# Hash-bucket attention and experts on one core: batch 0 visited once in float32, a planner that knows shared PSUM banks, Z beside the values

## The chip, the cores and the metric

One core of a Trainium2 chip. The metric is the device time of one execution in microseconds (us), as the median of several runs. A profile comes from one further execution; its span, from the first to the last instruction, lies a little inside its own time.

## The reference

Attention over q, k, v of shape (4 batches, 8 heads, 768, 64). `proj` gives each query and key a 6-bit bucket by the signs of six products; a query sees only the keys of its own bucket. The output of all heads, as 3072 tokens of 512, goes through one expert layer of 2048.

```python
mask = q_bucket[:, :, :, None] == k_bucket[:, :, None, :]
scores = np.where(mask, scale * np.matmul(q, k.transpose(0, 1, 3, 2)), -1000000000.0)
scores = scores - np.max(scores, axis=-1, keepdims=True)
attn = np.exp(scores)
attn = attn / (np.sum(attn, axis=-1, keepdims=True) + 1e-09)
x = np.matmul(attn, v)            # then (B, S, H * D) as B * S tokens
h = x @ w_in
g = s * (np.maximum(h, 0.0) ** 2) + b
return g @ w_out
```

## The kernel before

Work is cut into **slots**: one head of one batch and a chunk of 256 of its 768 queries, 96 slots in all. A **visit** is a head with the chunks that are done in a row. In a slot, `scores` writes 6 key tiles of scores into three PSUM banks (leading products, line 537 in float32, line 539 in float32r, a format with fewer passes), VectorE takes the maximum over tiles (L544), TensorE transposes it into bank 4 (L548), VectorE reduces it (L550), TensorE transposes back (L552), VectorE writes a row of negative maxima (L558), a closing product adds it to the scores (L567 or L569), and ACT takes the exps (L574). `values` multiplies exps by v into bank 3 (L596 float32; L598 and L599 for exps split into two float32r halves by ACT L591 and POOL L592). The sum of exps, Z, comes from a column of ones beside v and a spreading matmul (L614, L615), from 64 columns of ones (L617), or from VectorE and a float32r product (L620 to L626). ACT reads Z and the values from the banks (L628, L630), VectorE adds the low half (L632). For two heads together follow a reciprocal (L636) and a write of x to a buffer in DRAM (`xd`).

**Batch 0** is visited twice. First come eight visits with chunk 0 alone, all in float32 from tiles EQ and EK, one pair per head, which lie in the space of the weights' later halves. Then eight visits with chunks 1 and 2: `resplit` makes float32r halves of the head's q and k (ACT L446 and L453, POOL L448 and L456, six DMAs), so scores are float32r, while exps and v stay float32. Batches 1 to 3 are visited head by head with three chunks, in float32r halves throughout; a head's q and k are transposed (L399) and split (L401, L402) in three pieces through the second half of bank 4, and hashed (L424 to L429).

**Weights** come as 32 pieces of 512 KB; `decode` turns each into two float32r halves (ACT L319, L320, L325; VectorE L321, L322; POOL L323, L330, L331). `FIRST` and `RATE` say how many are decoded per slot: 2 in the first eight slots, then 1, and a piece of the second half not before its head's tiles are free.

**Experts** (`moe`): per chunk of 256 tokens of a batch 8 pairs of steps, each 24 products of 256 columns (L673), relu, square and split (L678 to L681) and 12 products of 512 columns (L690); 12 chunks in all. A chunk can start when all eight heads of its batch have done it. They use banks 5 to 7.

**The order** is computed before anything is emitted. Every step is given to `Plan` with its engine, a cost, what it reads and writes, and a priority: ten times the slot's number for attention, 1e5 and more for experts, so that experts fill TensorE where no attention step is ready. `Plan.order` runs a list schedule with these costs, and each engine's instructions are emitted in that order. Banks 3 and 4 are known to it as independent halves (`("b", 3, i % 2)`, `("b", 4, 0)`, `("b", 4, 1)`).

```python
av, ak, zz = bank[:, 3, i % 2 * CH:(i % 2 + 1) * CH], ("b", 3, i % 2), bank[:, 4, 0:CH]
...
cols, o = slice(g * CH, (g + 1) * CH), bank[:, 4, CH:2 * CH]          # split, for batches 1 to 3
```

Of the kernel before, what the change touches and what calls it, by code (L numbers as in the profile page):

```python
# [22 lines left out]
EPS = 1e-9  # L23
# [7 lines left out]

class Plan:
# [3 lines left out]
    def __init__(self):  # L36
        self.steps = []
        self.writer = {}
        self.readers = {}
        self.soft = {}  # L40

    def add(self, eng, cost, fn, r=(), w=(), pr=0.0, lag=0.0):
        i = len(self.steps)
        deps = set()
        for k in r:
# [12 lines left out]

    def order(self):
# [8 lines left out]
        moved = 0.0  # L68
        open_ = {}
# [4 lines left out]
        while len(out) < n:  # L74
            best = None
            for e, lst in open_.items():
                if lst:
                    t = max(free.get(e, 0.0), min(ready[i] for i in lst))
# [4 lines left out]
            safe = [i for i in open_[e] if ready[i] <= t and other[i] + self.soft.get(i, CHAIN) <= t] if e == PE else []  # L83
            i = min(safe, key=rank) if safe else min((i for i in open_[e] if ready[i] <= t), key=rank)
            if not safe:
                i = min((j for j in open_[e] if ready[j] <= t + LOOK.get(e, 0.0) * self.steps[i][1] and rank(j) <= rank(i)), key=rank)
            open_[e].remove(i)
            eng, cost, fn, pr, lag, deps = self.steps[i]
            start = max(free.get(e, 0.0), ready[i])
# [7 lines left out]
            out.append((start, i))  # L97
            for u in users[i]:
# [15 lines left out]
OFF = 0.4  # L114
LOOK = {DVE: 0.5, ACT: 0.0, POOL: 0.0}
# [3 lines left out]
def lsh_attention_moe(ctx: ExitStack, tc, q, k, v, proj, w_in, w_out, s, b, out):  # L119
# [50 lines left out]
    def mmc(n, c):  # L170
        return c * (n / 2325.0 + 0.0095)
# [6 lines left out]
    AQ = [tile_(f"aq{x}", [P, S], F32R) for x in range(2)]  # L178
    BQ = [tile_(f"bq{x}", [P, S], F32R) for x in range(2)]
    KS = [tile_(f"ks{x}", [P, 2, S], F32R) for x in range(2)]  # L180
# [9 lines left out]
    EQ = [wk.tile([P, WB], F32, tag=f"w{16 + 2 * h}", name=f"eq{h}") for h in range(H)]  # L190
    EK = [wk.tile([P, WB], F32, tag=f"w{17 + 2 * h}", name=f"ek{h}") for h in range(H)]
# [13 lines left out]
    rb = tile_("rb", [P, 2 * CH])  # L205
# [14 lines left out]
    for h in range(H):  # L220
        for e in (EQ[h], EK[h]):
            nc.vector.memset(e[:, S + (VA - 1) * VW + D:], 1.0)
            nc.vector.memset(e[:, S:S + (VA - 1) * VW].rearrange("p (t d) -> p t d", d=VW)[:, :, D:], 1.0)
    for h in range(H):
# [37 lines left out]
    for ks in KS:  # L262
        nc.vector.tensor_copy(ks[0:TPC, 1], ones[0:TPC].broadcast_to([TPC, S]))
# [13 lines left out]
    for cs in ((0,), tuple(range(1, NCH))):  # L277
        for h in range(H):
            visit(0, h, cs)
    for bb in range(1, B):  # L280
# [4 lines left out]
    preps = [w for w, z in enumerate(visits) if z["bb"] or w < H]  # L285
# [13 lines left out]
    def decode(u, pr):  # L299
# [15 lines left out]
        x = f"e{(u - 16) // 2}"  # L315
        plan.add(None, 0.0, new, [], rk + ([] if u < 16 else AK(x) if u % 2 == 0 else KK(x)) + [("vs", x, u % 2)], pr - 5)

# [15 lines left out]
    def bias(pr):  # L333

        cs = bank[:, 4, :]
        pe(0.9, lambda: nc.tensor.matmul(cs, ones.broadcast_to([P, P]), bcs, start=True, stop=True), ["bcs"], [("b", 4, 0), ("b", 4, 1)], pr)
        dve(512, lambda: nc.vector.tensor_scalar(bcs, cs, b_sb, None, ALU.mult), [("b", 4, 0), ("b", 4, 1), "sb"], ["bcs"], pr)
# [31 lines left out]
    def prep(w, i, pr):  # L369

        x, y, h, exact = visits[w]["x"], w % 2, visits[w]["h"], w < EARLY
        aq, bq, ks, nat = EQ[h] if exact else AQ[y], BQ[y], KS[y], NAT[y]
# [7 lines left out]
        def both(g, i, pr):  # L380

            pb = fill_bank()
# [5 lines left out]
            pe(0.33, tr, NK, [("b", pb)], pr)  # L388
            act(HS, lambda: nc.scalar.activation(aq[:, cols], o, AF.Copy, scale=qk_sb), [("b", pb)], AK(x, g=thirds(g)), pr, 0.12)
            dve(HS, lambda: nc.vector.tensor_copy(EK[h][0:D, cols], o[D:P]), [("b", pb)], [("ks", x, g)], pr, 0.5)  # L390
# [3 lines left out]
        def split(g, i, pr):  # L394
            cols, o = slice(g * CH, (g + 1) * CH), bank[:, 4, CH:2 * CH]

            def tr():
                for t in range(TPC):
                    nc.tensor.transpose(out=bank[:, 4, CH + t * P:CH + (t + 1) * P], in_=nat[:, g * TPC + t], identity=ident)  # L399
            pe(0.23, tr, NK, [("b", 4, 1)], pr)  # L400
            act(CH, lambda: nc.scalar.activation(aq[:, cols], o, AF.Copy, scale=qk_sb), [("b", 4, 1)], AK(x, g=(g,)), pr, 0.12)  # L401
            dve(CH, lambda: nc.vector.scalar_tensor_tensor(bq[:, cols], o, qk_sb, f32(aq[:, cols]), ALU.mult, ALU.subtract), [("b", 4, 1)] + AK(x, g=(g,)), BK(x, g=(g,)), pr, 0.48)  # L402
            if g == NCH - 1:
# [404 lines left out]
```

## Time and profile before

| | us |
|---|---|
| median of 3 runs | 1097.95 (1096.74 to 1098.52) |
| the profiled execution | 1100.34 |
| its span | 1098.5 |
| TensorE busy | 1042.3 |
| ScalarE (ACT) busy | 697.6 |
| GpSimd (POOL) busy | 688.9 |
| VectorE (DVE) busy | 654.8 |

PE is TensorE's matmuls, PEld its weight loads, which run beside matmuls. A matmul's record includes its latency, so in a dense run the records overlap, and a float32 matmul leaves two records. The granted clock is a share of 2.4 GHz. "<-" behind an idle time names what ended it.

### The profile page before, as it was taken

What the parts mean: (1) busy time and instruction counts of PE and PEld (TensorE: products, weight loads), DVE (VectorE), ACT (ScalarE), POOL (GpSimd) and SP (SyncE); (2) the same over time, 40 slices, a digit from 0 to 9 for tenths busy, and PEclk for the clock granted to TensorE, in tenths of its full rate; (3) what the DMA queues carried; (4) which work ended last, traced back from release to release, by engine and by line L of the source; (5) the groups of instructions that cost most, each with busy time, mean ns of one, the idle gap of its engine ahead of it and who ended that gap; (6) DMA issues with size and microseconds to landing.
All of it is one profiled execution on the core that took longest, in us unless ns stands there. A gap on an engine that the chain in (4) does not pass through costs nothing.

```text
span 1098.5 us, 18882 instructions
## 1 busy us (share of the span) xinstructions
PE 1042.3 (95%) x6862; PEld 924.3 (84%) x6862; DVE 654.8 (60%) x826; ACT 697.6 (64%) x1377; POOL 688.9 (63%) x622
## 2 busy tenths in 40 slices
PE   7998787899999999999999999999999999999998
PEld 5776665778889998889898888889898998999997
DVE  6776666566867777777777676768677753000000
ACT  4776666666777777676777776767676765233332
POOL 5466789666777767676776776757676865222221
PEclk9998889899999999999999999999999999999999
DMA  7663445323332432332432242333232211101010
GB/s 168 174 183 117 126 133 159 103 64 92 97 75 58 118 83 67 102 91 64 111 84 73 63 131 54 83 93 102 51 107 76 61 40 48 39 20 58 1 48 20
DMA packets 99404, 94.49 MB, mean 86 GB/s; under 512 B 68528, under 2 KB 72112, under 8 KB 99312
## 3 DMA queue, kind: packets, MB, share of 16 engines
q1 hardware_dynamic: 94112, 76.24, 26.1%
q10 hardware_dynamic: 5200, 17.05, 5.2%
q8 instruction: 54, 0.88, 0.3%
q14 instruction: 38, 0.31, 0.1%
HBM read 49.81 MB, written 18.87 MB: 63 GB/s over the span
## 4 chain that ended last, share of the span: by engine, by line
PE 73%; DVE 5%; ACT 2%; issue 2%; DMA 1%; POOL 0%; DVEq 0%; ACTq 0%
PE bank L673 23%; PE bank L690 21%; PE bank L569 5%; PE bank L539 5%; PE bank L598 4%; PE bank L599 4%; PE bank L548 2%; DVE mx L544 2%; PE bank L626 2%; PE bank L399 1%; PE bank L596 1%; PE bank L552 1%; DVE nat L429 1%; DVE zb L620 1%; PE bank L424 1%
## 5 line engine op out<-in xcount | busy, mean ns | idle before, releaser
L592 POOL TENSOR_TENSOR hl<-et,hl 128x512 fp32r<-128x512 f32 x216 | 278.1, 1317 | 126.2 <-ACT hl L591 101.0
L673 PE MATMUL bank<-xc,w 128*128 128x256 f32 x2304 | 339.3, 286 | 2.3 <-DMA xc<-xd 2.1
L673 PEld LDWEIGHTS bank<-xc,w 128*128 128x128 f32 x2304 | 304.5, 191 | 9.6 <-DMA xc<-xd 2.5
L690 PE MATMUL bank<-w,ghb 128*128 128x512 f32 x768 | 258.9, 402 | 0.0
L681 POOL TENSOR_TENSOR glb<-rb,ghb 128x512 fp32r<-128x512 f32 x96 | 125.1, 1303 | 133.7 <-ACT ghb L680 123.4
L544 DVE TENSOR_REDUCE mx<-bank 128x256 f32<-128x1536 f32 x96 | 168.4, 1754 | 52.1 <-PE bank L539 34.9
L620 DVE TENSOR_REDUCE zb<-et 128x256 f32<-128x1536 f32 x72 | 126.0, 1750 | 64.7 <-ACT et L574 61.8
L574 ACT ACTIVATE et<-bank 128x512 f32<-128x512 f32 x240 | 131.2, 621 | 49.3 <-PE bank L569 38.8
L690 PE MATMUL bank<-w,glb 128*128 128x512 f32 x384 | 154.6, 403 | 0.0
L690 PEld LDWEIGHTS bank<-w,ghb 128*128 128x128 f32 x768 | 136.0, 189 | 16.9 <-issue 0.3
L678 ACT ACTIVATE rb<-bank 128x512 f32<-128x512 f32 x96 | 57.3, 597 | 140.4 <-PE bank L673 136.4
L591 ACT CAST hl<-et 128x512 fp32r<-128x512 f32 x216 | 129.6, 661 | 0.9
L539 PE MATMUL bank<-aq,ks 78*128 78x256 f32 x528 | 120.8, 313 | 4.0 <-ACT ex L574 2.2
L598 PE MATMUL bank<-hl,vs 128*128 128x256 f32 x432 | 116.0, 289 | 0.3 <-ACT hl L591 0.3
L599 PE MATMUL bank<-hl,vs 128*128 128x256 f32 x432 | 113.2, 283 | 2.1 <-POOL hl L592 2.0
L539 PEld LDWEIGHTS bank<-aq,ks 78*128 78x128 f32 x528 | 92.0, 197 | 16.2 <-ACT ex L574 3.6
L698 DVE SCALAR_TENSOR_TENSOR osb<-bank,misc,bcs 128x512 f32<-128x512 f32 x22 | 16.0, 745 | 127.6 <-PE bank L690 127.5
L569 PE MATMUL bank<-bq,ks 128*128 128x256 f32 x528 | 81.0, 290 | 11.3 <-DVE bq L558 10.9
L599 PEld LDWEIGHTS bank<-hl,vs 128*128 128x128 f32 x432 | 82.1, 190 | 7.2 <-POOL hl L592 2.8
L569 PEld LDWEIGHTS bank<-bq,ks 128*128 128x128 f32 x528 | 71.1, 192 | 17.9 <-DVE bq L558 9.0
L636 DVE RECIPROCAL zpb<-zpb 128x256 f32<-128x256 f32 x48 | 83.7, 1744 | 3.2 <-ACT zpb L628 2.8
L598 PEld LDWEIGHTS bank<-hl,vs 128*128 128x128 f32 x432 | 82.1, 190 | 4.1 <-ACT hl L591 0.7
(115 smaller groups left out, 1631.5 us busy)
## 6 DMA issues: line engine op xcount, KB each, us to landing
xd<-xsb SPq DMA_DIRECT2D x48, 256.0 KB
xc<-xd SPq DMA_DIRECT2D x48, 256.0 KB
raw<-in_moe_w_in_dram ACTq DMA_DIRECT2D x16, 512.0 KB
raw<-in_moe_w_out_dram ACTq DMA_DIRECT2D x16, 512.0 KB
nat<-in_q_dram SPq DMA_DIRECT2D x32, 192.0 KB
nat<-in_k_dram SPq DMA_DIRECT2D x32, 192.0 KB
bq<-aq SPq DMA_DIRECT2D x32, 192.0 KB
out_dram<-osb SPq DMA_DIRECT2D x22, 256.0 KB
```

The costliest lines, as they stand in the source:

```text
L539: nc.tensor.matmul(o, ks[0:HR + TPC, 0, kt], aq[0:HR + TPC, cs], start=m == 0, stop=m == 1, skip_group_check=True)
L544: dve(S * TPC, lambda: nc.vector.tensor_reduce(t, sc, AX.XY, ALU.max), [("b", b) for b in pb], [tk], pr, 1.75)
L569: nc.tensor.matmul(o, ks[:, 1, kt], bq[:, cs], start=False, stop=m == 1, skip_group_check=True)
L574: act(512, lambda p=p, z=z: nc.scalar.activation(et(z) if plain(i) else pairs(z), bank[:, pb[p]] if plain(i) else bank[:, pb[p]].rearrange ...
L591: act(512, lambda z=z, y=y: nc.scalar.copy(HL[2 * y].rearrange("p (m n) -> p m n", n=CH), pairs(z)), [("e", z)], [("hl", 2 * y)], pr)
L592: pool(512, lambda z=z, y=y: nc.gpsimd.tensor_tensor(HL[2 * y + 1].rearrange("p (m n) -> p m n", n=CH), pairs(z), f32(HL[2 * y]).rearrange ...
L598: nc.tensor.matmul(av, VS[w % 2][:, kt], HL[2 * y][:, ms], start=(kt == 0), stop=False)
L599: nc.tensor.matmul(av, VS[w % 2][:, kt], HL[2 * y + 1][:, ms], start=False, stop=(kt == NT - 1))
L620: dve(S * TPC, lambda: nc.vector.tensor_reduce(ZB, es, AX.XY, ALU.add), [("e", z) for z in range(NE)], ["zb"], pr, 1.75)
L673: nc.tensor.matmul(hp, wt[("wi", n, cc)][:, m % 2, fs], xc[:, m // 2, :], start=(cc == 0 and m == 0), stop=(cc == NC_ - 1 and m == 2))
L681: pool(2 * CH, lambda r=r, gh=gh, gl=gl: nc.gpsimd.tensor_tensor(gl, r, f32(gh), ALU.subtract), [rk, hk], [lk], MP)
L690: nc.tensor.matmul(bank[:, 6 + t, :], (gh, gh, gl)[n][:, ts], wt[("wo", f)][:, n % 2], start=(f == 0 and n == 0), stop=(f == NF - 1 and n ...
```

## The change

Batch 0 is visited once, head by head with three chunks like the other batches, but wholly in float32: its 24 slots go the way that its first eight went (L537, L567, L596, L614, L615). Three sets of float32 tiles (q, k, v with a column of ones) take turns; they lie in the space that batches 1 to 3 later use for AQ, BQ, KS[1], VS and `rb`, and a set's heirs wait until batch 0's last head in that set is done (`freed`, at slots 18 and 24). `resplit` is gone. Odd slots of batch 0 keep their scores in banks 5 to 7 (`ODD`), so two slots' scores can stand at once; experts begin at slot 23 (`GATE`). Weights are decoded at 1.4 a slot from the start.

The planner learns two things. An engine's use of bank 3 or 4 is put after every other engine's use of that bank. And groups of steps hold a bank: between `hold(b)` and `hold(None)` a group's steps exclude other groups in bank `b`; while a slot's max is placed, only its own group or one that is more urgent by `BEHIND` may take bank 4.

Z moves from bank 4 to the second half of bank 3, beside the values, which no longer alternate between halves. Queries and keys are prepared in two pieces of 384 in place of three of 256, in the whole of bank 4. The cost model of 4-pass matmuls gets closer constants.

```diff
+    def hold(self, b):
+        self.now = (b, len(self.steps)) if b is not None else None
...
+        def clear(i, e):
+            b = self.half.get(i)
+            t = max([t for (n, o), t in used.items() if n == b and o != e], default=-9.0)
+            if i in self.lock and self.lock[i][0] not in holder:
+                t = max(t, again.get(self.lock[i][0], -9.0))
+            return t
+
+        def may(i):
+            if i not in self.lock:
+                return True
+            b, g = self.lock[i]
+            return holder.get(b, g) == g and (b != 4 or g in soon or g in holder.values() or all(self.steps[i][3] + BEHIND <= self.steps[j][3] for j in soon))
...
-    EQ = [wk.tile([P, WB], F32, tag=f"w{16 + 2 * h}", name=f"eq{h}") for h in range(H)]
-    EK = [wk.tile([P, WB], F32, tag=f"w{17 + 2 * h}", name=f"ek{h}") for h in range(H)]
+    NSET = 3
+    HQ = [wk.tile([P, S], F32, tag=f"aq{x}", name=f"hq{x}") for x in range(2)]
+    HK = [wk.tile([P, S], F32, tag=f"bq{x}", name=f"hk{x}") for x in range(2)]
+    H2 = wk.tile([P, 2, S], F32, tag="ks1", name="h2")
+    HV = [wk.tile([P, NT * 2 * D], F32, tag=f"vs{x}", name=f"hv{x}") for x in range(2)] + [rb]
...
-        visits.append({"bb": bb, "h": h, "x": len(visits) % 2 if bb or len(visits) >= H and h in SPLIT else f"e{h}"})
+        visits.append({"bb": bb, "h": h, "x": len(visits) % 2 if bb else f"e{(h + 1) % NSET}"})
...
-    for cs in ((0,), tuple(range(1, NCH))):
-        for h in range(H):
-            visit(0, h, cs)
-    for bb in range(1, B):
+    for bb in range(B):
         for h in range(H):
             visit(bb, h, tuple(range(NCH)))
...
         def split(g, i, pr):
-            cols, o = slice(g * CH, (g + 1) * CH), bank[:, 4, CH:2 * CH]
+            cols, o = slice(g * HS, (g + 1) * HS), bank[:, 4, 0:HS]
...
+            plan.hold(4)
...
-    def resplit(w, i, pr):
...
+        plan.hold(4)
+        plan.soon[len(plan.steps) - 1] = plan.now[1]
...
-        av, ak, zz = bank[:, 3, i % 2 * CH:(i % 2 + 1) * CH], ("b", 3, i % 2), bank[:, 4, 0:CH]
+        av, ak, zz = bank[:, 3, 0:CH], ("b", 3, 0), bank[:, 3, CH:2 * CH]
+        plan.hold(3)
...
-        elif exact:
-            zs, zk = av[D:P], [ak]
...
+        if i in AHEAD:
+            freed(AHEAD.index(i))
+            parts = parts + prep(H + AHEAD.index(i), i, pr)
...
-FIRST = 2
-RATE = 1.0
+FIRST = 1.4
+RATE = 1.4
+AHEAD = (18, 24)
-ODD = ()
-GATE = 0
+ODD = tuple(range(1, 24, 2))
+GATE = 23
```

## Rows read from the trace of the kernel before

**Rows 1.** The page's first part: busy us of each engine, share of the span, instructions.
```profile
PE 1042.3 (95%) x6862; PEld 924.3 (84%) x6862; DVE 654.8 (60%) x826; ACT 697.6 (64%) x1377; POOL 688.9 (63%) x622
```
**Rows 2.** Busy time by stretch: the stretch (us from the span's start) and its length, busy us and instructions of each engine, granted clock, share of the DMA engines, GB/s.
```profile
20.00:92.00 72.00, 67.44 (x365) 53.62 (x363) 52.27 (x73) 50.92 (x100) 39.26 (x33) 0.95 0.62 164
92.00:228.00 136.00, 108.58 (x552) 89.98 (x553) 86.84 (x96) 89.79 (x171) 107.73 (x87) 0.87 0.45 129
228.00:915.00 687.00, 671.17 (x4722) 606.34 (x4720) 493.08 (x583) 488.07 (x995) 484.86 (x450) 1.00 0.31 81
```
**Rows 3.** The same view for line 673 alone (experts, 256 columns): PE and PEld.
```profile
228.00:915.00 687.00, 228.31 (x1467) 197.20 (x1468) 1.00 0.31 81
915.00:1098.50 183.50, 94.92 (x740) 93.79 (x738) 0.99 0.10 34
```
**Rows 4.** The same for line 690 (experts, 512 columns).
```profile
228.00:915.00 687.00, 222.24 (x732) 125.16 (x732) 1.00 0.31 81
915.00:1098.50 183.50, 95.87 (x384) 69.47 (x384) 0.99 0.10 34
```
**Rows 5.** The chain that ended last, in order of time: start, us, what, number of records; three dense runs.
```profile
198.47 1.73 PE bank L596 x8
...
922.43 2.87 PE bank L673 x24
925.30 2.80 PE bank L690 x12
```
**Rows 6.** TensorE in order of time at the start: start, us, line, operation, records, idle time before.
```profile
10.80 0.91 PE L415 MATMUL bank<-eq,pj 128*128 128x384 f32 x2 [1.28 <-DMA nat<-in_k_dram]
11.55 0.82 PE L387 MATMUL bank<-ident,nat 128*128 128x128 f32 x6
```
**Rows 7.** TensorE in order of time, around one float32 slot: the same columns.
```profile
48.17 2.86 PE L537 MATMUL bank<-eq,ek 128*128 128x256 f32 x12
...
53.67 0.59 PE L596 MATMUL bank<-ex,ek 128*126 128x256 f32 x2
54.10 0.49 PE L387 MATMUL bank<-ident,nat 128*128 128x128 f32 x3
...
55.28 0.51 PE L480 MATMUL bank<-ones,eq 128*64 128x1 f32 x6
55.65 0.49 PE L480 MATMUL bank<-ones,ek 128*64 128x1 f32 x6
56.64 0.97 PE L567 MATMUL bank<-zhl,oner 128*128 128x256 f32 x6 [0.50 <-DVE zhl L558]
...
57.92 2.83 PE L537 MATMUL bank<-eq,ek 128*128 128x256 f32 x12
```
**Rows 8.** VectorE in order of time: the max (L544) of the first slot and of the eighth.
```profile
18.26 1.76 DVE L544 TENSOR_REDUCE mx<-bank 128x256 f32<-128x1536 f32 x1 [2.04 <-PE bank L537]
...
91.63 1.76 DVE L544 TENSOR_REDUCE mx<-bank 128x256 f32<-128x1536 f32 x1 [0.73 <-PE bank L537]
```
**Rows 9.** Groups of TensorE's instructions from 228 to 915 us: count, busy us, mean ns, idle time before; the transposes.
```profile
L548 PE MATMUL bank<-ident,mx 128*128 128x128 f32 x146 | 30.3, 289 | 6.0 <-ACT aq L401 2.2 <-DVE nat L429 1.7 <-DVE bq L402 1.4
...
L399 PE MATMUL bank<-ident,nat 128*128 128x128 f32 x138 | 26.9, 276 | 0.5 <-DVE nmt L550 0.4
...
L552 PE MATMUL bank<-ident,nmt 128*2 128x128 f32 x74 | 20.1, 271 | 3.2 <-DVE bq L402 1.5 <-DVE nat L429 1.1 <-ACT aq L401 0.3
```
**Rows 10.** Who TensorE's weight loads waited for from 228 to 915 us: us in total, times, longest.
```profile
PEld bank L548 <- DVE nat L429: 6.6, 15, 0.7
PEld bank L552 <- DVE bq L402: 4.9, 14, 0.9
PEld bank L548 <- DVE bq L402: 4.8, 13, 0.9
PEld bank L548 <- ACT aq L401: 3.7, 7, 0.8
```
**Rows 11.** Who TensorE's matmuls waited for in the same stretch.
```profile
PE bank L548 <- ACT aq L401: 2.2, 6, 0.6
...
PE bank L548 <- DVE nat L429: 1.7, 7, 0.3
```
**Rows 12.** Groups of ACT's instructions over the whole span: count, busy us, mean ns, idle time before.
```profile
L574 ACT ACTIVATE et<-bank 128x512 f32<-128x512 f32 x240 | 131.2, 621 | 49.3 <-PE bank L569 38.8 <-POOL glb L681 6.4 <-PE bank L567 2.0
...
L630 ACT ACTIVATE xpb<-bank,vmn 64x256 f32<-64x256 f32 x96 | 44.9, 467 | 55.1 <-PE bank L599 54.3
L628 ACT ACTIVATE zpb<-bank 64x256 f32<-64x256 f32 x96 | 36.3, 378 | 28.4 <-PE bank L596 15.9 <-DVE nat L429 6.0 <-PE bank L399 2.3
...
L319 ACT ACTIVATE osb<-raw 128x512 f32<-128x512 f32 x32 | 21.5, 671 | 8.0 <-POOL w L331 5.7 <-DMA raw<-in_moe_w_in_dram 1.2 <-POOL bcs L330 0.7
L320 ACT ACTIVATE raw<-raw 128x512 int32<-128x512 uint32 x32 | 21.4, 669 | 0.0
L325 ACT CAST w<-osb 128x512 fp32r<-128x512 f32 x32 | 19.6, 619 | 9.2 <-POOL osb L323 9.2
...
L389 ACT ACTIVATE eq<-bank,misc 128x384 f32<-128x384 f32 x16 | 9.0, 578 | 7.2 <-PE bank L387 5.3 <-DVE ek L390 1.9
...
L420 ACT COPY ek<-eq 12x768 f32<-12x768 f32 x8 | 6.6, 828 | 1.4 <-DVE eq L417 1.2
...
L614 ACT ACTIVATE zb<-bank 1x256 f32<-1x256 f32 x8 | 3.0, 376 | 11.4 <-PE bank L596 11.3
```

More of the change, by code (lines that the diff above doesn't have):

```diff
@@ L40, in __init__ @@
         self.soft = {}
+        self.half = {}
+        self.lock = {}
+        self.now = None
+        self.size = {}
+        self.soon = {}
     def add(self, eng, cost, fn, r=(), w=(), pr=0.0, lag=0.0):
         i = len(self.steps)
+        if self.now:
+            self.lock[i] = self.now
+            self.size[self.now[1]] = self.size.get(self.now[1], 0) + 1
         deps = set()
+        for k in list(r) + list(w):
+            if isinstance(k, tuple) and k[0] == "b" and len(k) == 3:
+                self.half[i] = k[1]
         for k in r:
@@ L75, in order @@
             best = None
-            for e, lst in open_.items():
+            for e, every in open_.items():
+                lst = [i for i in every if may(i)]
                 if lst:
-                    t = max(free.get(e, 0.0), min(ready[i] for i in lst))
+                    t = max(free.get(e, 0.0), min(max(ready[i], clear(i, e)) for i in lst))
                     if best is None or t < best[0]:
@@ L97, in order @@
             out.append((start, i))
+            if i in self.soon:
+                soon.append(self.soon[i])
+            if i in self.lock:
+                b, g = self.lock[i]
+                holder[b] = g
+                todo[g] -= 1
+                until[b] = max(until.get(b, -9.0), end)
+                if not todo[g]:
+                    again[b] = until[b]
+                    if g in soon:
+                        soon.remove(g)
+                    del holder[b]
+            if i in self.half:
+                used[self.half[i], e] = end
             for u in users[i]:
@@ L114 @@
 OFF = 0.4
+BEHIND = 8.0
 LOOK = {DVE: 0.5, ACT: 0.0, POOL: 0.0}
@@ L284, in lsh_attention_moe @@
     EARLY = H
-    preps = [w for w, z in enumerate(visits) if z["bb"] or w < H]
+    preps = list(range(len(visits)))
     w_in_w = w_in.bitcast(I32)
@@ L469, in prep_values @@
+        plan.hold(None)
     def prep_values(w, pr):
         bb, h = visits[w]["bb"], visits[w]["h"]
-        x = visits[w]["x"] if bb else f"e{h}"
+        x = visits[w]["x"]
         vk = [("vs", x, 0), ("vs", x, 1)]
@@ L497, in prep_values @@
         pool(NT * D, lambda: nc.gpsimd.tensor_tensor(VS[y][:, :, 1, :], to, f32(VS[y][:, :, 0, :]), ALU.subtract), ["vn", vk[0]], vk[1:2], pr)
-        if not bb:
-            return
         dve(NT * D, lambda: nc.vector.tensor_reduce(pj[:, 0:D], to.rearrange("p t d -> p d t"), AX.X, ALU.add), ["vn"], ["vp"], pr, 0.84)
-        pe(0.25, lambda: nc.tensor.matmul(bank[0:D, 4, CH:CH + 1], pj[:, 0:D], ones, start=True, stop=True), ["vp"], [("b", 4, 1)], pr)
+        plan.hold(4)
+        pe(0.25, lambda: nc.tensor.matmul(bank[0:D, 4, 0:1], pj[:, 0:D], ones, start=True, stop=True), ["vp"], [("b", 4, "m")], pr)
         mean(bb, h, pr)
     def plain(i):
-        return not slots[i][0] and (i < EARLY or slots[i][1] in PLAIN)
+        return not slots[i][0]
     def et(z):
@@ L708, in lsh_attention_moe @@
     todo = []
-    def ok(g, i):
-        w = H + g
-        d = 2 if g in SPLIT else 0
-        return max(j for j in range(NSL) if slots[j][3] == w - d) + 1 + d // 2 <= i
     def decodes(i):
-        if i < EARLY:
-            return min(ND // 2, int(FIRST * (i + 1)))
-        n = int(FIRST * EARLY + RATE * (i - EARLY + 1))
-        free = sum(max(j for j in range(NSL) if slots[j][3] == w - d) + 1 + d // 2 <= i for w in range(H, 2 * H) for d in [2 if visits[w]["h"] in SPLIT else 0])
-        free = min([free] + [g for g in range(H) if not ok(g, i)])
-        return min(n, ND // 2 + 2 * free)
+        return min(ND, int(FIRST * min(i + 1, H) + RATE * max(0, i - H + 1)))
     for w in preps[:2]:
@@ L751, in lsh_attention_moe @@
         one = i + 2 >= NSL or slots[i + 2][3] != slots[i + 1][3]
-        now, parts = (parts, []) if not last or one else (parts[:2], parts[2:])
+        now, parts = (parts[:2], parts[2:]) if not bb or last and not one else (parts, [])
         values(i, pr + 5, now)
@@ L778 @@
 EP = -4
-PLAIN = (0, 1, 2, 3, 4, 5, 6, 7)
 MP = 1e4
```

186 lines of the change are left out of this document (104 added, 82 removed).

## The prediction

> **What bounds the kernel now.** I read the page's busy times first, then busy time by stage, then the two lines of the expert part in the same stages, and only then single waits. The page gives TensorE 95% of the span [rows 1], but that is an average over unlike stages. By stage: from 915 us on the clock is 0.99 and nothing but expert products runs [rows 3, 4]; from 228 to 915 it is busy for 671 of 687 us at 1.00; from 92 to 228 it is busy for 109 of 136 us [rows 2] at a granted clock of 0.87, between its two levels, 1.2 and 2.4 GHz, and that is where time lies idle. Busy time flatters TensorE, since a matmul's record covers its latency, so I price its work by the spacing in dense runs [rows 5]: 24 products with 256 columns in float32r take 2.87 us, 0.119 each; 12 with 512 columns 2.80, 0.233 each; 8 records with 256 columns in float32 1.73, 0.216 each, and a float32 matmul leaves two records. A 128-column transpose I take at half of a 256-column product, 0.06.
>
> With these prices each stage splits into work and loss. The tail, 915 to 1098.5, holds 740 and 384 expert products [rows 3, 4]: 88.1 + 89.5 = 177.6 us of work, 5.9 lost. The middle, 228 to 915, holds 4722 records [rows 2], of which 1467 + 732 are expert products [rows 3, 4], 174.6 + 170.6 = 345.2 us; 146 + 138 + 74 = 358 are transposes [rows 9], 21.5 us; the other 2165 at 0.119 are 257.6 us. That is 624.3 us of work and 62.7 lost. The first 228 us hold all of batch 0 but the last slot's values, and little of the expert work.
>
> **The change, part by part.** The sum is made against the profiled execution: span 1098.5, its own time 1100.34 (1.84 around the span), and the median of the runs shown, 1097.95, lies 2.4 below that.
>
> *More TensorE work.* All 24 slots of batch 0 become what its first eight are now. The other 16 have their 6 leading and 6 closing score products in float32r, 12 x 0.119 = 1.43 us; they get 12 float32 records and 6 closing ones, 12 x 0.216 + 6 x 0.119 = 3.31. That is 1.88 x 16 = 30.1 us. Each also gets the one float32 matmul that spreads Z, 2 x 0.216 = 0.43, 6.9 us. So 37 us are added, and the change must win that back from losses.
>
> *Batch 0 by itself.* A float32 slot's own work: 2.59 (lead) + 0.71 (close) + 2.59 (values) + 0.43 (Z) + 3 x 0.06 = 6.50 us. A head's preparation: 4 records of 384 columns, 1.5 x 0.216 each, 1.30; 6 transposes, 0.36; 12 sums of v at 6 in 0.37 us [rows 7], 0.74; together 2.40. 24 x 6.50 + 8 x 2.40 = 175.2, and the first head of batch 1, 6 transposes and 9 products, 1.4, is prepared there too: 176.6. The start loses about 9.9: dense work begins at 11.55, after a wait for k's load [rows 6], with 6 transposes and 4 records of head 0 done before, 1.7 us; this start stays, since heads 0 and 1 are prepared as now. Per slot, the present float32 stage shows the loss: from one set of lead products to the next 9.75 us pass [rows 7] with 6.50 + 2.40 = 8.90 of work, 0.85 lost. The upper end is the mean from the first max to that of slot 7, (91.63 - 18.26) / 7 = 10.48 [rows 8], 1.58 lost. The lower end, 0.3, is an estimate: the wait of 0.50 us for the row of maxima before the closing products [rows 7] gone. After the change a slot has only a third of a head to fill gaps, but the next slot's scores stand in three other banks and can always run. These two pull against each other, so I take 0.8, next to the row of the same slots: 19.2 us. Expert work can only follow when slot 23's exps have freed bank 5 and the last weights are decoded; for this handover no row exists: nothing at best, and at worst 6 us, an estimate for one chain with nothing behind it (max 1.76 [rows 8], 3 exps at 0.62 [rows 12], row steps and hand-overs in between). I take the middle, 3. Batch 0 then ends at 176.6 + 9.9 + 19.2 + 3 = 208.7 us, with no expert work done.
>
> *The re-splitting goes.* The second visits' copies, subtractions and six DMAs a head leave ACT, POOL and SP. They stand in the stretch that lost most, so their removal is inside the new batch-0 sum and not counted again. One load of v per head in place of three on SP: nothing, it comes six slots ahead. Decoding is spread over 23 slots at 1.4 a slot; it is not on TensorE's path as long as ACT has room (a rival below).
>
> *The order with one engine per bank.* In the middle stage weight loads wait for engines with which they share bank 4 and no data: L548 for L429, L402 and L401, L552 for L402, 6.6 + 4.9 + 4.8 + 3.7 = 20.0 us [rows 10]; TensorE itself idles 2.2 + 1.7 = 3.9 us for two of them [rows 11]. So 3.9 to 23.9 us can go; load waits overlap running matmuls in part, so I take the middle, 14, and the loss of the middle falls from 62.7 to 48.7. What is late next are the true steps of the chain (max, row, exps), which expert products cover. Preparing in two pieces in place of three leaves columns and price as they are: 0.
>
> *Z beside the values.* Bank 3 now belongs to one slot from its first value product to its last read. Queued behind on TensorE are the next slot's value products, and behind those the expert products' rank, not their data. In batches 1 to 3 expert products cover that: 0. If that cover ran out, which needs a pace above about 10.1 us a slot (136 us of experts per batch over 24 slots, 5.65, plus 4.5 of attention with losses), against 687 / 72 = 9.5 now, each further us would cost 24 per batch. The added wait at slot 24 (keys of batch 1's second head only when head 7's are free) has three slots before its use: 0.
>
> *The sum.* 208.7 + all 96 expert pairs, 96 x (24 x 0.119 + 12 x 0.233) = 542.6, + attention of batches 1 to 3, 279.1 less slot 23's 24 records (2.9) and the head prepared earlier (1.4), 274.8, + 48.7 + 5.9 = **1080.7** for the span. Plus 1.84, less 2.4: **1080** us. With all low ends (0.3, 0, 23.9) the span is 1056; with all high ends (1.58, 6, 3.9) 1113.
>
> **Rivals.**
> *A. The values' bank drains in the open* (slower). Place: slots 0 to 23, where no expert products stand behind. After the last value product ACT reads Z (0.376), TensorE spreads it (0.43), ACT reads again (0.378) and adds the mean (0.467) [rows 12]: 1.65 us in which no other value product may start. All of it bare would cost 24 x 1.65 = 39.6 us: **1120**. It decides against the change once more than 17.8 / 24 = 0.74 us a slot is bare beyond my 0.8. For it: today the halves of bank 3 alternate, and now only one slot's group may be open. Against it: in the row of a present slot TensorE goes on from the last values to other work without a wait [rows 7], and the next slot's scores are such work. The Trainium skill, page Perfetto Trace Analysis, section Matmuls, speaks for A: independent groups should rotate through banks, so that one's evacuation runs beside the next one's products; no run here shows a float32 slot with that bank in one hand. Chance 0.08.
> *B. The order's model and the chip part ways.* If instructions drift from their planned times, bank waits return under other names and the float32 slots lose as much as the mean of the first eight: middle 62.7 and half-way to 1.58 (1.2): +14 + 9.6, **1104**; with the middle's loss alone **1094**. For it: the plan of today knows the max, row and read steps and still loses 62.7. Chance 0.17, half of it below the kernel's present time.
> *C. ScalarE sets batch 0's pace.* Per slot 3 exps (1.86), 0.376, 0.378, 0.467, 32/24 decodes of 0.671 + 0.669 + 0.619 (2.61) and a third of a head's 2 x 0.578 + 0.828 (0.66) [rows 12]: 6.35 us. Of my slot of 8.1 us that is 78%; the present float32 stage has 71% [rows 2]. At 71% a slot takes 8.94, +20 us: **1100**. Against it: nothing there shows ACT as the limit. Chance 0.09.
> *D. Two slots in flight hide nearly everything*: low ends, **1056**. For it: TensorE is never out of score products. Chance 0.08.
>
> **How the numbers follow.** My case has 0.58, and holds 1064 to 1095. The range 1054 to 1111 takes in B, C and D and leaves A and the ends out. A measurement of this kernel can tell about 0.2% from no change (1095.8 to 1100.1 is "same"). Faster: 0.58 + 0.08 + 0.08 (half of B) + 0.01 of C = 0.75. Same: 0.03 of B, 0.04 of C: 0.07. Slower: A, the rest of B and C: 0.18.
>
> **What would show it.** Right: no expert product before some 205 us, all 32 decodes by then; maxes of slots 2 to 23 spaced 7.5 to 8.5 us; a clock near 1.00 from 25 to 200 us, against 0.87 now; L596 and L537 with 288 records each; waits of the transposes for bank 4's other readers all but gone; a tail of expert products longer than now, near 200 us. Wrong: spacing above 9 us in batch 0 (A, if value products wait for ACT; C, if ACT is busy over 85%); transposes that still wait some 20 us in the middle (B); a hole of over 6 us between the last slot of batch 0 and the first expert product.

## The result, and the profile after

The changed kernel takes 1072.46 us (median; 1071.75 to 1073.04) against 1097.35 for the kernel before in the same comparison: a ratio of 0.9772, 95% interval 0.9755 to 0.9789, or 24.9 us saved. The profiled execution took 1071.75 us with a span of 1070.0. The forecast was 1080.

Lines have moved: L537 is now L576, L539 L578, L544 L583, L548 L589, L552 L593, L558 L600, L574 L617, L591 and L592 L636 and L637, L596 L641, L598 and L599 L643 and L644, L614 and L615 L662 and L663, L626 L674, L628 L677, L630 L679, L399 L459, L402 L463, L429 L493, L673 L723, L678 L728, L690 L740. First the page's busy times, which answer to [rows 1].

```profile
PE 1044.6 (98%) x6918; PEld 936.2 (87%) x6918; DVE 634.7 (59%) x750; ACT 686.3 (64%) x1355; POOL 652.0 (61%) x593
```

TensorE is as busy as before in us, in a span 28.5 us shorter. By stage, as [rows 2], cut where the slots themselves mark it: max of slot 0 to max of slot 23, on to that of slot 27, on to that of slot 95, and the rest.

```profile
17.30:194.70 177.40, 171.94 (x928) 142.45 (x927) 130.71 (x167) 127.92 (x254) 105.27 (x88) 1.00 0.44 130
194.70:234.70 40.00, 33.33 (x212) 28.64 (x212) 27.13 (x31) 29.64 (x60) 34.20 (x31) 0.98 0.32 87
234.70:896.10 661.40, 654.88 (x4623) 600.02 (x4623) 451.28 (x500) 460.54 (x927) 458.14 (x423) 1.00 0.30 81
896.10:1070.00 173.90, 170.28 (x1085) 153.42 (x1084) 16.19 (x19) 60.66 (x103) 50.06 (x43) 1.00 0.10 34
```

Batch 0 now has TensorE busy for 172 of 177 us at a granted clock of 1.00, where its second part had 109 of 136 at 0.87 [rows 2]. The expert lines in the same four stretches, L723 and then L740, answer to [rows 3, 4].

```profile
17.30:194.70 177.40, 0.00 (x0) 0.00 (x0) 1.00 0.44 130
194.70:234.70 40.00, 9.48 (x59) 8.41 (x59) 0.98 0.32 87
234.70:896.10 661.40, 241.17 (x1561) 210.60 (x1561) 1.00 0.30 81
896.10:1070.00 173.90, 88.08 (x688) 86.67 (x687) 1.00 0.10 34
```
```profile
234.70:896.10 661.40, 235.29 (x780) 133.57 (x780) 1.00 0.30 81
896.10:1070.00 173.90, 90.51 (x360) 64.96 (x360) 1.00 0.10 34
```

No expert product runs in batch 0. The middle does 1561 + 780 of them.

The loss is the stretch less its work at the forecast's prices; products of 384 columns and sums of one column, which it had not priced apart there, count 0.18 and 0.067. For 234.7 to 896.1: experts 185.8 + 181.7; 336 transposes 20.2; 132 products of 384 columns 23.8; 44 sums 2.9; the other 1770 records 210.6; together 625, so 36 of 661 us are lost. The same slots of the kernel before:

```profile
268.80:903.30 634.50, 621.24 (x4395) 562.80 (x4394) 457.39 (x542) 453.50 (x926) 448.51 (x417) 1.00 0.31 83
```

With 1367 and 684 expert products, 334 transposes, 44 sums and 1966 others that is 579, and 56 lost. Summed record by record, both kernels divide so:

| us | work, whole span | lost to slot 0's max | slots 0 to 23 | 23 to 27 | 27 to 95 | tail | all |
|---|---|---|---|---|---|---|---|
| before | 958.1 | 8.5 | 65.4 of 215.0 | 3.2 | 55.7 | 7.7 | 140.4 |
| after | 995.3 | 7.4 | 16.3 of 177.4 | 11.1 | 35.8 | 4.0 | 74.7 |

So 37.2 us of work were added and 65.7 us of loss removed: 49 in batch 0, 20 in the middle, 5 at the two ends, less 8 given back at the hand-over (slots 23 to 27, from batch 0 to batch 1). Two views show where. VectorE's maxes (L583), first, second and last of batch 0:

```profile
17.26 1.76 DVE L583 TENSOR_REDUCE mx<-bank 128x256 f32<-128x1536 f32 x1 [1.18 <-PE bank L576]
21.68 1.74 DVE L583 TENSOR_REDUCE mx<-bank 128x256 f32<-128x1536 f32 x1
...
194.68 1.74 DVE L583 TENSOR_REDUCE mx<-bank 128x256 f32<-128x1536 f32 x1
```

Slot 1's max starts 4.4 us after slot 0's; the mean spacing is (194.68 - 17.26) / 23 = 7.71 us, against 9.35 before with 21.8 us of expert work in it. And the largest waits of weight loads from 234.7 to 896.1, to be laid beside [rows 10]:

```profile
PEld bank L644 <- POOL hl L637: 2.5, 3, 1.3
PEld bank L589 <- DVE mx L583: 2.0, 3, 1.3
PEld bank L589 <- ACT hl L636: 1.5, 1, 1.5
```

The 20.0 us for engines with which the transposes share a bank and no data are gone. The first two rows that are left, the values' products for the exps' low halves and the transposes for the maxima, are true steps of the chain; the third is a single wait for an engine whose result the transpose does not read.

### The profile page after: what moved, and what is told of

Same layout as the page of the kernel before. It is cut to its first block, busy times and chain, and to the rows that moved or that the text cites. A ratio compares the mean times of both kernels' runs of the same rounds, so it can differ in the third digit from the quotient of the medians.

```text
span 1070.0 us, 18632 instructions
## 1 busy us (share of the span) xinstructions
PE 1044.6 (98%) x6918; PEld 936.2 (87%) x6918; DVE 634.7 (59%) x750; ACT 686.3 (64%) x1355; POOL 652.0 (61%) x593
## 4 chain that ended last, share of the span: by engine, by line
PE 87%; DMA 3%; POOL 3%; ACT 3%; issue 2%; DVE 2%; ACTq 0%; SPq 0%; DVEq 0%; POOLq 0%
PE bank L723 25%; PE bank L740 23%; PE bank L644 5%; PE bank L612 5%; PE bank L643 5%; PE bank L641 4%; PE bank L578 4%; PE bank L576 4%; PE bank L589 2%; DMA xd<-xsb 2%; PE bank L674 2%; PE bank L610 1%; PE bank L459 1%; POOL hl L637 1%; DMA raw<-in_moe_w_out_dram 1%
## 5 line engine op out<-in xcount | busy, mean ns | idle before, releaser
L637 POOL TENSOR_TENSOR hl<-et,hl 128x512 fp32r<-128x512 f32 x216 | 279.1, 1319 | 139.8 <-ACT hl L636 123.1
L723 PE MATMUL bank<-xc,w 128*128 128x256 f32 x2304 | 338.7, 285 | 1.1 <-DMA xc<-xd 0.7
L723 PEld LDWEIGHTS bank<-xc,w 128*128 128x128 f32 x2304 | 305.7, 191 | 9.3 <-DMA xc<-xd 0.9
L740 PE MATMUL bank<-w,ghb 128*128 128x512 f32 x768 | 258.9, 401 | 0.0
L583 DVE TENSOR_REDUCE mx<-bank 128x256 f32<-128x1536 f32 x96 | 168.1, 1751 | 16.8 <-PE bank L578 12.2
L740 PE MATMUL bank<-w,glb 128*128 128x512 f32 x384 | 153.5, 401 | 0.1
L617 ACT ACTIVATE et<-bank 128x512 f32<-128x512 f32 x240 | 132.5, 624 | 32.8 <-PE bank L612 21.0
L740 PEld LDWEIGHTS bank<-w,ghb 128*128 128x128 f32 x768 | 136.3, 189 | 17.9 <-issue 0.8
L728 ACT ACTIVATE rb<-bank 128x512 f32<-128x512 f32 x96 | 57.5, 599 | 144.6 <-PE bank L723 134.7
L636 ACT CAST hl<-et 128x512 fp32r<-128x512 f32 x216 | 131.4, 667 | 0.4
L643 PE MATMUL bank<-hl,vs 128*128 128x256 f32 x432 | 118.6, 294 | 1.0 <-ACT hl L636 0.6
L644 PE MATMUL bank<-hl,vs 128*128 128x256 f32 x432 | 113.8, 282 | 1.9 <-POOL hl L637 1.9
L679 ACT ACTIVATE xpb<-bank,vmn 64x256 f32<-64x256 f32 x96 | 44.9, 468 | 74.9 <-PE bank L644 74.0
L578 PE MATMUL bank<-aq,ks 78*128 78x256 f32 x432 | 86.8, 290 | 3.2 <-DMA aq<-nat 3.1
L644 PEld LDWEIGHTS bank<-hl,vs 128*128 128x128 f32 x432 | 82.3, 191 | 7.0 <-POOL hl L637 2.5
L643 PEld LDWEIGHTS bank<-hl,vs 128*128 128x128 f32 x432 | 82.1, 190 | 6.8 <-ACT hl L636 1.0
L740 PEld LDWEIGHTS bank<-w,glb 128*128 128x128 f32 x384 | 72.4, 189 | 11.7 <-POOL glb L731 0.6
L578 PEld LDWEIGHTS bank<-aq,ks 78*128 78x128 f32 x432 | 69.8, 190 | 9.8 <-ACT zhl L667 3.3
```

The lines of the kernel that those rows point to most:

```text
L578: nc.tensor.matmul(o, ks[0:HR + TPC, 0, kt], aq[0:HR + TPC, cs], start=m == 0, stop=m == 1, skip_group_check=True)
L583: dve(S * TPC, lambda: nc.vector.tensor_reduce(t, sc, AX.XY, ALU.max), [("b", b) for b in pb], [tk], pr, 1.75)
L617: act(512, lambda p=p, z=z: nc.scalar.activation(et(z) if plain(i) else pairs(z), bank[:, pb[p]] if plain(i) else bank[:, pb[p]].rearrange ...
L636: act(512, lambda z=z, y=y: nc.scalar.copy(HL[2 * y].rearrange("p (m n) -> p m n", n=CH), pairs(z)), [("e", z)], [("hl", 2 * y)], pr)
L637: pool(512, lambda z=z, y=y: nc.gpsimd.tensor_tensor(HL[2 * y + 1].rearrange("p (m n) -> p m n", n=CH), pairs(z), f32(HL[2 * y]).rearrange ...
L643: nc.tensor.matmul(av, VS[w % 2][:, kt], HL[2 * y][:, ms], start=(kt == 0), stop=False)
```

## The experiments

Ratios are to the kernel before on the same chip, with their 95% interval.

**1. The changed kernel without the rule on banks.** The planner again ignores when another engine used a bank; everything else stays.

```diff
-            t = max([t for (n, o), t in used.items() if n == b and o != e], default=-9.0)
+            t = -9.0
```

> The changed kernel, but the planner no longer puts an engine's use of bank 3 or 4 after other engines' uses of that bank (the groups that hold a bank stay). Theory (the planner's knowledge of shared banks is what cut the middle's loss by some 25 us): waits of the transposes for other readers of bank 4 return and the time rises by 12 to 25 us, to 1085-1097. Rival (fewer and larger pieces in bank 4, and Z moved out of it, are what cut the loss; knowing the times adds nothing): within 4 us of the changed kernel, 1070-1076.

Measured 1100.14, ratio 1.0024 [1.0008, 1.0041]. Batch 0 is untouched (16.4 lost, spacing 7.67); slots 27 to 95 lose 57.5, as before the change. The first waits of its weight loads there:

```profile
PEld bank L674 <- ACT xpb L679: 10.6, 19, 0.6
PEld bank L589 <- DVE nat L493: 5.2, 2, 2.7
PEld bank L578 <- ACT et L617: 4.4, 13, 0.6
```

The spread of Z (L674) waits for the read of the values (L679), which now shares its bank: the waits come back under another name, as rival B described. Only 5.2 us are waits of the transposes in bank 4, which my expectation had put first. Within this kernel the rule is worth 27.7 us, and without it the rest of the change gains nothing.

**2. The kernel before with that rule alone.**

```diff
+            return max([t for (n, o), t in used.items() if n == b and o != e], default=-9.0)
...
-            start = max(free.get(e, 0.0), ready[i])
+            start = max(free.get(e, 0.0), at[i])
...
+            if i in self.half:
+                used[self.half[i], e] = end
```

> The kernel before, with that one thing added to its planner: a step that uses bank 3 or 4 is put after other engines' uses of that bank. No groups, no new order of batch 0, Z where it was. Theory: it wins most of the middle's 25 us by itself, 1075-1085. Rival: without groups and without the freed bank 4 it wins little, 1092-1098.

Measured 1099.17, ratio 1.0011 [0.9991, 1.0032]: no gain. Batch 0 loses 6 less, slots 40 to 47 lose 28.3. There (440 to 480 us) no expert product is in the trace at all, and all of TensorE's work is this:

```profile
440.00:460.00 20.00, 15.27 (x76) 12.59 (x74) 11.80 (x16) 9.67 (x21) 10.05 (x10) 0.67 0.32 84
460.00:480.00 20.00, 14.36 (x63) 12.20 (x63) 13.08 (x16) 10.84 (x22) 10.67 (x11) 0.59 0.25 63
```

The experts of batch 0 ran out before batch 1 was through. Priced record by record, all of their 136 us were done by slot 44; the kernel before had done 117 by then and 130 by slot 47, when batch 1's own experts were about to start, so it had next to nothing to spare. Outside slots 40 to 47 the middle of this run loses 36, against 49 in the same slots before. So the rule pays only where expert work lasts; neither the rule nor the rest without it (experiment 1) pays alone.

**3. One slot's scores at a time in batch 0.**

```diff
-ODD = tuple(range(1, 24, 2))
+ODD = ()
```

> The changed kernel with all scores of batch 0 in banks 0 to 2, so that one slot's scores stand at a time (ODD empty). Theory (the next slot's scores are what fills TensorE in batch 0, since no expert products are there): slots of batch 0 are spaced 8.7 to 9.5 us in place of 7.7, and the time rises by 24 to 43 us, to 1096-1115. Rival (preparing heads and values fills the gaps, as in the kernel before's first eight slots): spacing below 8.2, time below 1085.

Measured 1099.41, ratio 1.0019 [1.0003, 1.0035]. Batch 0 goes to a spacing of 9.28 and loses 48.8, 32.5 more; slots 27 to 95 lose 34.0, no more than in the changed kernel. Stretch and weight loads' waits of its batch 0:

```profile
17.00:231.00 214.00, 191.98 (x957) 151.03 (x956) 140.50 (x174) 136.71 (x272) 122.17 (x101) 0.97 0.40 114
```
```profile
PEld bank L663 <- ACT xpb L679: 13.0, 17, 1.1
PEld bank L593 <- DVE nmt L591: 12.2, 19, 1.3
PEld bank L610 <- DVE zhl L600: 6.5, 11, 1.2
```

In the changed kernel the same three waits are 2.0, 2.5 and 1.5. With one slot in flight nothing covers the row of maxima and the reads of bank 3, and the second set of score banks is what covers them. The 13.0 us lie inside rival A's drain, but it is the spread of Z that waits for the read of the values, not, as A had it, the next slot's value products.

**4 and 5. Z back in bank 4.** First with the values in alternating halves, then with Z's place alone changed.

```diff
-        av, ak, zz = bank[:, 3, 0:CH], ("b", 3, 0), bank[:, 3, CH:2 * CH]
+        av, ak, zz = bank[:, 3, i % 2 * CH:(i % 2 + 1) * CH], ("b", 3, i % 2), bank[:, 4, 0:CH]   # 4
+        av, ak, zz = bank[:, 3, 0:CH], ("b", 3, 0), bank[:, 4, 0:CH]                             # 5
-        plan.hold(3)       # 4 alone
...
+            plan.hold(4)       # around Z's product and its read
```

> The changed kernel with Z back in bank 4 (its product and its read by ACT as a group that holds bank 4) and the values alternating between halves of bank 3 again, not held. Theory (Z beside the values matters little for TensorE; it clears bank 4 for the chain): time 1072-1082, chains later as Z waits for bank 4. Rival A of the prediction (one bank for values and Z drains in the open in batch 0): this version is faster than the changed kernel, by 5 us or more, with batch 0's slots closer than 7.7 us.

Measured 1130.43, ratio 1.0288 [1.0252, 1.0324]. Rival A's reading, that values alternating again would help, falls; my own 1072 to 1082 was wrong by 50 us as well.

> The changed kernel with Z's product and its read back in bank 4, as a group that holds it; the values stay in the first half of bank 3 and hold it. Theory (a third kind of group in bank 4 delays either Z or the chain, and with it the reads that free bank 3): most of the loss of the version with Z back and values alternating, 1105-1130. Rival (that loss came from the values' alternating halves, whose accumulation is cut by the other half's readers): 1072-1085.

Measured 1137.9, ratio 1.0368 [1.0348, 1.0389]. So Z's place, with the hold that goes with it, makes the loss. Batch 0 goes to 8.48 us a slot, slots 27 to 95 to 10.79, above the 10.1 from which the forecast let the experts run short, and they do. L723 from 680 to 800 us:

```profile
680.00:720.00 40.00, 12.36 (x77) 10.65 (x77) 0.98 0.30 79
720.00:760.00 40.00, 5.88 (x29) 4.99 (x29) 0.72 0.29 76
760.00:800.00 40.00, 14.58 (x95) 12.58 (x94) 1.00 0.18 44
```

Bank 4 then serves transposes, preparation and Z, each shutting the others out, which fits the longer pace but is argued, not shown; a run with Z in bank 4 but not held was not made, so how much is the hold's and how much the bank's stays open.

**6. The second head of batch 1 prepared earlier**, its tiles freed at slot 21 by moving the third float32 set elsewhere.

```diff
-    H2 = wk.tile([P, 2, S], F32, tag="ks1", name="h2")
+    late["gh"] = wk.tile([P, 2, 2 * CH], F32, tag="gh", name="h2q")
+    late["gl"] = wk.tile([P, 2, 2 * CH], F32, tag="gl", name="h2k")
...
-AHEAD = (18, 24)
+AHEAD = (18, 21)
```

> The changed kernel with the third set's q and k in the space of the experts' ghb and glb in place of KS[1], so that batch 1's second head can be prepared from slot 21 and not from slot 24. Theory (the hand-over from slot 23 to 27 loses some 11 us mostly because that head's preparation, its DMAs included, comes late and all at once): the stretch from slot 23's max to slot 27's loses under 6 us and the time falls by 4 to 8 us, to 1064-1069. Rival (the hand-over is slow because value splitting starts on ACT and POOL while the last decodes run): no change beyond 2 us.

Measured 1064.86, ratio 0.9708 [0.9687, 0.9729]. The time was as the theory said, the place was not: slots 23 to 27 still lose 11.7. The gain stands in batch 0 (2.8) and the middle (5.6), and at the hand-over an expert product now waits for the load of its chunk's x:

```profile
212.76 1.13 PE L723 MATMUL bank<-xc,w 128*128 128x256 f32 x4 [2.43 <-DMA xc<-xd]
```

**7. Decoding at 2 a slot** (`FIRST` and `RATE` 2.0 for 1.4).

> The changed kernel with weights decoded at 2 a slot in batch 0 in place of 1.4, so that ACT, VectorE and POOL are fuller in slots 0 to 15 and emptier after. Theory (TensorE sets batch 0's pace, ACT has room): slots of batch 0 stay near 7.7 us and the time within 4 us of the changed kernel, 1068-1077. Rival C of the prediction (ACT is the limit): slots 0 to 15 go to 8.5 us or more, time 1078-1090.

Measured 1076.41, ratio 0.9809 [0.979, 0.9828]; spacing 8.11. The last piece is now copied at 173.9 us, in slot 18, and not after slot 23. From slot 0's max to slot 19's and on to slot 23's, first here, then in the changed kernel:

```profile
17.70:175.90 158.20, 147.53 (x784) 121.59 (x783) 122.45 (x149) 119.69 (x234) 110.42 (x92) 0.99 0.45 137
175.90:204.10 28.20, 28.00 (x148) 23.26 (x148) 15.41 (x21) 12.84 (x28) 6.53 (x7) 1.00 0.17 45
```
```profile
17.30:161.90 144.60, 141.20 (x773) 117.52 (x772) 104.04 (x132) 102.35 (x204) 82.11 (x69) 1.00 0.43 126
161.90:194.70 32.80, 30.74 (x156) 24.94 (x155) 26.67 (x35) 25.57 (x51) 23.16 (x20) 1.00 0.50 148
```

With the fuller engines a slot takes 8.33 us for 7.61, with ACT at 76% for 71%; with decoding over it takes 7.05 for 8.20, with TensorE busy throughout. So decoding does press on the slots, by more than the mean over batch 0 shows, but not to C's pace of 8.5 or to its 85% of ACT. Which of the three engines that decode it is, no run separates. Batch 0 loses 24.9 for 16.3 and the hand-over 6.0 for 11.1, so 4 us of it are left in the time.

**8. The old batch 0 with all the rest new**: two visits and re-splitting as before, but with the planner, the held groups, Z beside the values, two pieces and the new costs.

```diff
-            cols, o = slice(g * CH, (g + 1) * CH), bank[:, 4, CH:2 * CH]
+            cols, o = slice(g * HS, (g + 1) * HS), bank[:, 4, 0:HS]
...
+            plan.hold(4)
...
-        av, ak, zz = bank[:, 3, i % 2 * CH:(i % 2 + 1) * CH], ("b", 3, i % 2), bank[:, 4, 0:CH]
+        av, ak, zz = bank[:, 3, 0:CH], ("b", 3, 0), bank[:, 3, CH:2 * CH]
+        plan.hold(3)
```

> The kernel before in all that concerns batch 0 (two visits, re-splitting, experts from slot 8, one slot's scores at a time), with the rest of the change: planner with bank times and groups, Z beside the values, two pieces per head in bank 4, closer costs. Theory (the rest of the change cuts the loss of batches 1 to 3 by some 20 us wherever batch 0 is, and the new batch 0 pays little beyond its 37 us of extra work): 1074-1084. Rival (batch 0's new order brings most of the gain): 1088-1098.

Measured 1092.52, ratio 0.9943 [0.9922, 0.9964]. Slots 27 to 95 lose 60.5, of which 29.4 in slots 40 to 47; outside them 31, as in the changed kernel. Its 256-column expert products (L740 in that kernel) around the hole:

```profile
400.00:420.00 20.00, 6.10 (x45) 5.51 (x43) 1.00 0.44 117
420.00:440.00 20.00, 1.66 (x6) 1.37 (x6) 0.80 0.28 81
440.00:460.00 20.00, 0.00 (x0) 0.00 (x0) 0.69 0.17 41
460.00:480.00 20.00, 2.52 (x15) 2.07 (x15) 0.74 0.32 84
```

The old batch 0 uses 29 us of its own experts as filler, and batch 1 then lacks them: three chunks are 3 x 45.2 = 136 us, 5.65 a slot over batch 1's 24. All 136 were done by slot 44 here, as in experiment 2. The new batch 0 fills itself with a second slot and hands all 136 us on: in the changed kernel 103 of them were done by slot 44, 118 by slot 47.

**9. The same with `GATE = 23`**, to keep the experts of batch 0 for batch 1.

> The kernel before's batch 0 with the rest of the change, and experts held back to slot 23, as in the changed kernel. In the version without this hold, no expert product ran from about 422 to 462 us: the experts of batch 0 were used up before those of batch 1 could start, and slots 40 to 47 lost 29 us. Theory (the new batch 0 pays because it needs no experts to fill it, and so leaves all of batch 0's experts for batch 1): the hole is gone and batches 1 to 3 lose about 36 us as in the changed kernel, but batch 0, now unfilled, loses 20 to 30 us more; the time stays at 1082-1098. Rival (the hole is of another cause, or old batch 0 needs no filling either): the hole stays, or the time falls to 1072 or below.

Measured 1092.02, ratio 0.9949 [0.9931, 0.9966], and it decides nothing: the constant moved only the point where expert steps are handed to the planner, which ran them early all the same (162 products of 256 columns before 230 us), and slots 40 to 47 lose 29.9. (The hole in experiment 8's trace runs from 428.8 to 476.4 us, longer than the expectation has it.) In the changed kernel the order of the visits keeps experts back: head by head, a chunk of batch 0 has all its heads only in slots 21 to 23. Experiment 3 leaves banks 5 to 7 free in batch 0, and still only 9 expert products ran there:

```profile
17.00:231.00 214.00, 2.55 (x9) 1.64 (x9) 0.97 0.40 114
```

Whether truly late experts would close the hole in the old batch 0 was not tried.

**10. The old constants of the cost model.**

```diff
-        return c * (n / 2400.0 + 0.0013) if c % 4 == 0 else c * (n / 2325.0 + 0.0095)
+        return c * (n / 2325.0 + 0.0095)
```

> The changed kernel with the old cost of 4-pass matmuls in the planner (0.478 us for 256 columns where the chip takes 0.43). Theory (a small part of the change; waits in batch 0 shift a little): 1068-1080, no more than the two re-dealt orders differ. Rival (planned times must be close, since bank times are counted in them): over 1085.

Measured 1063.3, ratio 0.97 [0.9676, 0.9723]: faster than the changed kernel, so the closer constants bring nothing here. Of the 9 us, 7.7 stand at the hand-over, which loses 3.4 in this order, though slot 24 frees the same tiles. TensorE's waits there:

```profile
PE bank L641 <- ACT zpb L677: 0.3, 1, 0.3
PE bank L663 <- ACT xpb L679: 0.3, 1, 0.3
```

**11 and 12. Controls: the planner's hand-over time of TensorE** (`HOP`, 0.2) set to 0.21 and 0.19, to see what a re-dealt order alone does.

> The changed kernel with one constant of the planner's cost model moved by nothing that matters: 0.21 us in place of 0.20 from a TensorE step to its readers. It re-deals the order of all engines. Theory (the order's details move the time by a few us only): 1067-1078. Rival (the order is luck to the extent of tens of us, so that differences between the versions so far say little): outside 1060-1085.

Measured 1175.75, ratio 1.0719 [1.0686, 1.0753]. It is no fair control: with `HOP` above `SAME` (0.2, the credit for a step that follows on its own engine) each accumulating step counts as not ready for 0.01 us, and the planner mixes the two strands of the expert part. TensorE in the tail, and its waits over the whole span:

```profile
1000.97 1.20 PE L723 MATMUL bank<-xc,w 128*128 128x256 f32 x7 [0.75 <-ACT rb L728]
1002.29 0.50 PE L740 MATMUL bank<-w,ghb 128*128 128x512 f32 x1
1002.62 0.28 PE L723 MATMUL bank<-xc,w 128*128 128x256 f32 x1
```
```profile
PE bank L723 <- ACT rb L728: 30.9, 50, 0.7
```

Before, in the tail, 24 products of one kind stood in a row [rows 5]; here the first products wait for the relu that must empty their bank. In the tail, weight loads wait 34.2 us for it, most of the 46 us that the tail loses more than in the changed kernel; of the 53 more in slots 27 to 95 the larger part is unexplained.

> The same with 0.19 us. Theory 1067-1078; rival outside 1060-1085.

Measured 1066.12, ratio 0.9723 [0.9702, 0.9744]. A change that should mean nothing moves the time by 6 us. So differences of less than some 10 us between versions of the changed kernel (6, 7, 10 and 12: 1063 to 1076) are not put down to their edits; that figure is an estimate from these few orders, and 11 shows that a poor order can cost ten times as much. Experiments 1 and 3 to 5 lie well outside the 10 us, and the losses of 1 and 3 stand where their edits act (21.7 in slots 27 to 95, 32.5 in batch 0); 2 and 8, near the kernel before, are judged by their hole and not by their few us. Three of these versions, 6, 10 and 12, beat both kernels.

## Why the prediction was right

The forecast span was 1080.7, the measured one 1070.0. Split in its own terms, work 994.0 was forecast and 995.3 found; losses of 86.7 (9.9 + 19.2 + 3 + 48.7 + 5.9) were forecast and 74.7 found. So the terms were right and the sizes of single losses were off. All but the hand-over were put too high, by 2 to 13 us; that and the hand-over's 8 too low leave 11 us in the span and 8 in the time. A re-dealt order moves the time as much (experiments 10 and 12), so a hit this close is in part luck:

- **More work, 37 us:** 37.2. The prices from dense runs [rows 5] carried over to slots that did not exist yet, and L576 and L641 have the 288 records each.
- **Batch 0:** the slots were to come every 7.5 to 8.5 us; 7.71. The loss was 16.3 for 19.2. The clock is 1.00, as forecast. Experiment 3 shows what makes it so: one slot more in flight, 27 us of time.
- **The hand-over, 3 us:** right where the forecast looked, wrong behind it. From slot 23's max to the first expert product 1.6 us are lost, inside its bounds of 0 to 6 for one chain with nothing behind it. But the whole of slots 23 to 27 loses 11.1, against 3.2 before: behind the first expert product lies a string of small waits, of which TensorE's view shows the largest:

```profile
202.24 0.82 PE L723 MATMUL bank<-xc,w 128*128 128x256 f32 x4
...
211.70 0.44 PE L589 MATMUL bank<-ident,mx 128*128 128x128 f32 x2 [0.98 <-DVE bq L463]
...
232.28 0.47 PE L578 MATMUL bank<-aq,ks 78*128 78x256 f32 x2 [3.09 <-DMA aq<-nat]
```

The last is the load of batch 1's second head, which may start only when slot 24 frees its tiles. The forecast priced that wait at 0 with three slots before its use; it was 3.09. Experiment 6 moved it and the stretch still lost 11.7; experiment 10 left it where it was, and in another order the load came in time and the stretch lost 3.4. So the string belongs to this order and not to the freed tiles; what the planner would have to know to avoid it stays open.

- **The middle, 48.7:** 35.8 for slots 27 to 95; with slots 23 to 27, which the forecast's stretch took in, 46.9 for 51.7. The forecast took the middle of 3.9 to 23.9 us for the waits of [rows 10, 11]; 19.9 went in slots 27 to 95, near the upper end. If those waits are all of it, a weight load's wait was mostly lost time and not half covered; but the held groups and the two pieces came with the rule, and no run has them apart. Experiment 1 gives 21.7 back with the rule taken out. (Of the forecast's 62.7 for the stretch before, two slips cancel: 24 float32 records and 46 sums of one column were all priced at 0.119, some 2.3 us too low and too high.)
- **Z beside the values, 0:** right in sign, and its weight was missed. The forecast asked what Z costs in bank 3 and not what it would cost in bank 4 under the new rule, as a group that holds it: 58 and 65 us (experiments 4, 5). Its limit of 10.1 us a slot held: at 10.79 the experts ran short, at 9.73 they don't.
- **First expert product and decodes near 205:** 202.2; the last piece's copy on ACT (L379) starts at 209.1 and its last subtraction on POOL (L385) at 211.0, 4 to 6 us later than forecast.
- **The tail, near 200 us:** wrong, and it was not expert products alone (10 of the 1134 records from 915 us on are slot 95's values and Z). From slot 95's max it is 173.9 us, against 195.2 before, since slots 27 to 95 took in 1561 + 780 expert products at 9.73 us a slot, against 1367 + 684 at 9.33. Why the slots there came further apart stays open; where expert products stand does not change the sum of work.
- **What carried the gain into the middle** was not in the forecast. It put batch 0 and the order side by side as two sums, and that step was wrong, though the total was not: experiments 1, 2 and 8 show that they need each other. All but the rule gave 1100, the rule alone 1099, all but the new batch 0 1092.5. The new batch 0 alone, with the old planner and the old places, was not run.

Rival A: the drain of bank 3 exists, but in the changed kernel's batch 0 it is small. Weight loads of Z's spread wait 2.0 us for the read of the values, and those of value products (L641) 2.2 us for the read of Z (L677): under 0.2 us a slot, where A needed 0.74. The Trainium skill, page Perfetto Trace Analysis, section Matmuls, which spoke for A, advises that independent groups rotate through different banks. Alternating halves of one bank are not that, so experiment 4 does not test it; the odd slots' scores in banks 5 to 7 are, and there the page agrees with experiment 3: 27 us. Rival B's waits returned in experiment 1, where the planner did not count banks; that planned and real times part, which was B's reason, no run shows, and in the changed kernel's middle such waits come to 2.3 us at most (0.8 for Z's spread, 1.5 for the single wait named above). Rival C's pressure is real in experiment 7, and at 1.4 pieces a slot it stayed inside the forecast's 7.5 to 8.5 us. Of rival D's low ends the middle came near (19.9 of 23.9); batch 0, at 0.7 us a slot for 0.3, and the hand-over did not.

## What to carry to other kernels

A planner that orders by data alone pays for every PSUM bank that several engines share; count when the other engines leave the bank, and, as far as experiments 4 and 5 go, give each bank to few kinds of work. Filler work is a stock: look at where it runs out before asking how well it is used, since a stretch that fills itself can pay in the next one. Before crediting a few us to an edit in a listed order, move a constant that should mean nothing and see how far the time goes.

## What the runs showed of the hardware

Where experts ran out, TensorE was still busy for 15.44 of 20 us by its records, and the granted clock was 0.69, between its levels of 1.2 and 2.4 GHz; 60 us before, at 20.00 of 20, it was 1.00:

```profile
380.00:400.00 20.00, 20.00 (x143) 18.24 (x142) 13.11 (x16) 13.86 (x29) 13.18 (x13) 1.00 0.23 54
...
440.00:460.00 20.00, 15.44 (x76) 12.58 (x74) 11.95 (x15) 11.82 (x26) 10.45 (x10) 0.69 0.17 41
```

(These are rows of experiment 8.) One line of the values' products (L658 in that kernel) in the two stretches:

```profile
L658 PE MATMUL bank<-hl,vs 128*128 128x256 f32 x12 | 3.3, 296 | 0.0
...
L658 PE MATMUL bank<-hl,vs 128*128 128x256 f32 x13 | 4.9, 385 | 0.2 <-ACT hl L651 0.2
```

A hole thus costs twice, by the waits and by slower products beside them (385 ns a record for 296), and a busy share of 77% hides it; the loss against priced work does not.
